# A state-space scan feeding an MLP on one core: exponentials by head, a shorter weight decode, and another order of the MLP's blocks

## The chip, the cores and the metric

The kernel runs on one core of one Trainium2 chip. What counts is the device time of one execution in microseconds. The engines are named as in the profile: PE multiplies matrices, DVE and POOL work elementwise, ACT evaluates functions and copies, SP starts most transfers. PEld is PE's weight load. Each engine works off its own instructions in the order in which they were written; an instruction can wait for others by semaphores, and everything behind it on its engine then waits too.

## What is computed

For each of 4 batches and 8 heads, 768 tokens pass through a scan with a state of 16 x 32 numbers, and the result, rearranged to 3072 tokens of 256 numbers, passes through an MLP with 2048 hidden units:

```
la = log(clip(a, 1e-6, 1)); cum = cumsum(la) within a chunk
L  = exp(cum_i - cum_j) where i >= j, else 0
y  = ((C B^T) * L) x  +  (C state) * exp(cum)
state = exp(cum_last) * state + sum_j exp(cum_last - cum_j) B_j x_j
h  = y @ w_in;   g = h * clip(h + 3, 0, 6) / 6;   out = g @ w_out
```

The two weight matrices are float64 in DRAM. All other inputs and the output are float32.

## The kernel before

The scan uses chunks of 128 tokens instead of the reference's 32, so there are six. Chunk `c` of all four batches makes 512 tokens, and the MLP works through the same 512 tokens as block `k = c`. All tiles have 128 partitions.

*The weights.* They come in eight raw pieces of 1 MB (0 to 3 are `w_in`, 4 to 7 `w_out`), read as pairs of 32-bit words into one of two `raw` buffers. `decode_a` and `decode_b` rebuild a float32 from sign, exponent, and mantissa: `s` is the top 16 bits, `e` the exponent (two biased Relu passes on ACT), `m` the mantissa (scaled on ACT, its low word added on DVE); `decode_b` ends with the product, and asks for the raw piece two further on. Piece i of `w_in` is needed by hidden slices f = 4i to 4i + 3, piece 4 + i of `w_out` by the same slices of the second product.

*The attention part of a chunk* is a generator, `steps(c)`, whose pieces are woven into the MLP of the block before. `ends` makes `bs` (POOL), `eto` (ACT) and `tmp` (POOL); `turn(c, p)` transposes B and C of two batches into `t_ps` and copies them out as `bT` (ACT), `cT` and `csT` (DVE). `decay(c, b)` works on the tile `L`, into which `load_decay` has put the cumulated logs of batch b: POOL subtracts the row's own (L272) and masks (L273), ACT exponentiates (L276). `scores` makes four `cb` tiles on PE and multiplies them into `L` on DVE; `mix` sums into `y`, and `keep` copies `yT` (ACT) and forms the next state (DVE). Chunk 0 needs no transfer for `L`: `diff_first` makes the masked differences in PSUM, in tiles named `d`, with a bf16 mask product (L226), one product per head (L230) and one wide product with `ident_n` (L233), and `decay_first` exponentiates (L242).

*The MLP.* `mlp_in(k, f)` multiplies slice f into an `h` tile (L395), ACT makes `r` (L400), DVE makes slice f of `gT` (L401). One such step is two products in the program and four PE instructions in the trace. `mlp_out(k, b, ...)` sums the 16 slices for batch b into an `o` tile (L409): 16 products, 32 instructions. ACT copies it to `ob`, SP writes it out.

*Order.* It is written by hand: nothing is reordered. The first product of block k is followed by the second product of block k - 1, so two `gT` buffers live at once. Decodes 0 to 2 stand in the opening, 3 and 4 in block 0's first product, 5 to 7 in block 1's. `turn` of the next chunk stands after f = 9 and f = 13, the other pieces between the four `o`.

*Buffers.* PSUM has eight banks. The pool `ps` gives six to `d`, `c_ps`, `t_ps`, `cb`, `h` and `o` in turn, in the order of their making, and two hold `y`. A new tile waits until the readers of the tile that had its bank are done. The tiles `L` and four early ones share five buffers named `big`.

## Time and profile before

| | us |
|---|---|
| median of 3 runs | 473.97 (472.18 to 474.04) |
| profiled execution | 473.95 |
| its span, first to last instruction | 472.2 |
| busy: PE, DVE, ACT, POOL | 445.6, 161.6, 146.4, 75.6 |
| moved by DMA | 30.15 MB |

The span is 1.75 us less than the profiled execution's time; that difference is work around the span. The share of busy time says little here, since a matmul instruction counts as busy for as long as it lasts, and one of the same shape lasts twice as long in some stretches as in others. The chain of waits, read by stretches, says more. Rows of the profile give a line, an engine, an operation, what is written and read, the shape, and a count; in brackets stands how long the engine was idle before, and what ended that.

### The profile page before, as it was taken

To read this page: it belongs to the slowest core of one execution; us is meant where nothing else is said; L and a number is where in the kernel's file an instruction comes from. 1 tells how busy PE (TensorE), PEld (TensorE's weight loads), DVE (VectorE), ACT (ScalarE), POOL (GpSimd) and SP (SyncE) were. 2 spreads that over 40 slices of the span, in tenths; PEclk is the share of its full clock that TensorE was granted. 3 is DMA by queue.
4 is the path that set the end of the run, shared out by engine and by line. 5 is a ranking of instruction groups with operands and counts; after the bars stand their busy time and mean duration, and the time that the engine had idled before them with its cause. 6 is when DMAs were issued, how large, how long until landed. Compare 5 with 4: busy or idle time off the path is not lost.

```text
span 472.2 us, 5101 instructions
## 1 busy us (share of the span) xinstructions
PE 445.6 (94%) x2036; PEld 278.7 (59%) x2036; DVE 161.6 (34%) x291; ACT 146.4 (31%) x225; POOL 75.6 (16%) x63
## 2 busy tenths in 40 slices
PE   5999698999855999999999999999999999999997
PEld 3655343444312778545877446785458774488886
DVE  4514468384639221245121434212451114300000
ACT  5430564637544100345111344003451114400000
POOL 2000009200048000019000057232000000000000
PEclk9999999899985799999999999999999999999999
DMA  8706853148300032620112800326200000000000
GB/s 163 206 4 125 182 161 134 44 178 112 135 0 0 3 104 82 79 70 1 56 58 89 135 0 0 106 77 75 33 1 12 18 17 2 0 11 24 11 24 22
DMA packets 87048, 30.15 MB, mean 64 GB/s; under 512 B 75536, under 2 KB 81360, under 8 KB 87024
## 3 DMA queue, kind: packets, MB, share of 16 engines
q1 hardware_dynamic: 86800, 29.73, 26.3%
q8 instruction: 16, 0.26, 0.2%
q10 hardware_dynamic: 224, 0.10, 0.1%
q14 instruction: 8, 0.07, 0.0%
HBM read 26.57 MB, written 3.24 MB: 63 GB/s over the span
## 4 chain that ended last, share of the span: by engine, by line
PE 81%; issue 8%; DMA 3%; DVE 3%; POOL 2%; ACT 2%; SPq 0%; POOLq 0%; ACTq 0%
PE o L409 36%; PE h L395 26%; PE cb L327 4%; PE d L230 3%; PE y L356 3%; PE d L233 3%; PE y L350 2%; PE y L362 2%; DMA L<-cum_d 1%; POOL L L272 1%; DMA bc<-in_B_dram 1%; PE t_ps L305 1%; PE d L226 1%; DVE w_out L184 1%; DVE gT L401 1%
## 5 line engine op out<-in xcount | busy, mean ns | idle before, releaser
L395 PE MATMUL h<-yT,w_in 128*128 128x512 f32 x384 | 178.4, 619 | 6.6 <-DVE gT L401 5.1
L409 PE MATMUL o<-w_out,gT 128*128 128x256 f32 x768 | 173.5, 385 | 0.0
L409 PEld LDWEIGHTS o<-w_out,gT 128*128 128x128 f32 x768 | 145.9, 192 | 24.4 <-issue 4.1
L395 PEld LDWEIGHTS h<-yT,w_in 128*128 128x128 f32 x384 | 74.2, 198 | 97.5 <-issue 82.1
L401 DVE SCALAR_TENSOR_TENSOR gT<-r,h 128x512 f32<-128x512 f32 x96 | 64.4, 685 | 110.6 <-ACT r L400 110.4
L400 ACT ACTIVATE r<-h,half 128x512 f32<-128x512 f32 x96 | 63.8, 685 | 76.9 <-PE h L395 70.1
L335 DVE TENSOR_TENSOR L<-L,cb 128x256 f32<-128x256 f32 x96 | 33.9, 415 | 104.4 <-PE cb L327 101.2
L414 ACT COPY ob<-o 128x256 f32<-128x256 f32 x24 | 8.9, 372 | 143.1 <-PE o L409 137.6
L272 POOL TENSOR_TENSOR L<-L,cum_t 128x1024 f32<-128x1024 f32 x20 | 39.7, 1987 | 19.6 <-DMA L<-cum_d 19.6
L327 PE MATMUL cb<-cT,bT 32*128 32x256 f32 x192 | 27.9, 484 | 4.2 <-DVE gT L401 3.8
L284 POOL TENSOR_TENSOR bs<-bc,e_from 128x512 f32<-128x512 f32 x5 | 5.3, 1057 | 164.0 <-DMA bc<-in_B_dram 152.0
L276 ACT ACTIVATE L<-L 128x1024 f32<-128x1024 f32 x20 | 21.2, 1061 | 18.4 <-POOL L L273 18.4
L377 ACT COPY yT<-y 128x256 f32<-128x256 f32 x24 | 7.8, 375 | 55.4 <-PE y L362 46.9
L327 PEld LDWEIGHTS cb<-cT,bT 32*128 32x128 f32 x192 | 12.8, 209 | 20.4 <-issue 9.0
L273 POOL TENSOR_SCALAR_AFFINE_SELECT L<-L 128x1024 f32<-128x1024 f32 x20 | 23.6, 1181 | 1.5
L356 PE MATMUL y<-L,xt 128*32 128x128 f32 x384 | 18.4, 303 | 3.1 <-DVE L L335 3.1
L230 PE MATMUL d<-cum,ident 32*128 32x128 f32 x64 | 16.6, 436 | 3.8 <-DVE cum L195 3.8
L230 PEld LDWEIGHTS d<-cum,ident 32*128 32x128 f32 x64 | 14.2, 323 | 8.2 <-DVE cum L195 4.4
L356 PEld LDWEIGHTS y<-L,xt 128*32 128x32 f32 x384 | 10.3, 116 | 8.8 <-DVE L L335 3.9
L233 PE MATMUL d<-ident_n,cum 32*128 32x512 f32 x16 | 15.3, 1056 | 0.0
L293 POOL TENSOR_TENSOR tmp<-state,eto 128x512 f32<-128x512 f32 x4 | 4.2, 1052 | 59.5 <-ACT eto L290 59.5
L380 DVE TENSOR_TENSOR state<-y,mask 128x256 f32<-128x256 f32 x10 | 4.2, 424 | 25.6 <-ACT yT L377 25.6
(58 smaller groups left out, 177.4 us busy)
## 6 DMA issues: line engine op xcount, KB each, us to landing
L<-cum_d SPq DMA_DIRECT2D x20, 512.0 KB, 3.8
raw<-in_moe_w_in_dram SPq DMA_DIRECT2D x4, 1024.0 KB, 5.4
raw<-in_moe_w_out_dram SPq DMA_DIRECT2D x4, 1024.0 KB, 5.4
xt<-in_x_dram SPq DMA_DIRECT2D x6, 512.0 KB, 6.9
out_dram<-ob SPq DMA_DIRECT2D x24, 128.0 KB, 1.7
bc<-in_C_dram SPq DMA_DIRECT2D x6, 256.0 KB, 5.7
bc<-in_B_dram SPq DMA_DIRECT2D x6, 256.0 KB, 7.6
eto<-cum_d SPq DMA_DIRECT2D x40, 32.0 KB, 2.9
```

The source lines that it names most:

```text
L230: nc.tensor.matmul(out=d[:, q], lhsT=ident[:rows, g + q:g + q + 1].to_broadcast([rows, P]), rhs=cum[:, 0], start=False, stop=True, skip_gr ...
L233: nc.tensor.matmul(out=d, lhsT=cum[:, 0], rhs=ident_n[:, g:g + HU].unsqueeze(2).to_broadcast([rows, HU, P]), start=False, stop=True, skip_ ...
L272: nc.gpsimd.tensor_tensor(out=L, in0=L, in1=by_j, op=ALU.subtract)
L273: nc.gpsimd.affine_select(out=L, in_=L, pattern=[[0, NH], [1, P]], compare_op=ALU.is_ge, fill=-1e5, base=0, channel_multiplier=-1)
L276: nc.scalar.activation(L, L, AF.Exp)
L327: nc.tensor.matmul(out=cb.rearrange("j h i -> j (h i)"), lhsT=bT[rows, b % 2], rhs=cT[rows, b % 2].rearrange("n t i -> n (t i)"), start=Tr ...
L335: nc.vector.tensor_tensor(out=L[:, hs], in0=L[:, hs], in1=cbs[q], op=ALU.mult)
L356: nc.tensor.matmul(out=y_ps[u][32 * q:32 * q + 32, k], lhsT=xt[:, b * NH + h], rhs=L[:, h], start=(c == 0), stop=True, tile_position=(0, 3 ...
L395: nc.tensor.matmul(out=h, lhsT=w_in[:, j, f * P:(f + 1) * P], rhs=yTs[k][:, j].rearrange("p b i -> p (b i)"), start=(j == 0), stop=(j == N ...
L400: nc.scalar.activation(r, h, AF.Relu, bias=half, scale=1.0 / 6.0)
L401: nc.vector.scalar_tensor_tensor(out=gTs[k][:, f], in0=r, scalar=1.0, in1=h, op0=ALU.min, op1=ALU.mult)
L409: nc.tensor.matmul(out=o, lhsT=gTs[k][:, f, b * P:(b + 1) * P], rhs=w_out[:, f], start=(f == 0), stop=(f == NF - 1))
```

## The change

The exponentials take the row's own cumulated log as a bias, negated in `cum_n`. In chunk 0 the wide product L233 goes, and 32 passes of 128 x 128 (`decay_exp`) take the place of eight of 128 x 512. In chunk 1, POOL's subtraction goes, and eight such passes for each batch take the place of one of 128 x 1024. Later chunks subtract on POOL as before.

The decode has three parts now. `decode_a` copies `s` and masks `m`, `e` and `s`, and makes the exponent in one Relu pass that writes bf16; `decode_b` merges exponent and sign and adds the low word; `decode_c` multiplies. The mantissa's scaling pass on ACT is gone. Three `raw` buffers hold pieces, and a piece is asked for after `decode_b`. One function table is loaded at the start.

Block k's second product now follows its own first product, so one `gT` buffer serves. Decodes 0 and 1 stand in the opening, 2 to 5 in block 0's first product, 6 and 7 between its first and second. In block 0 the batches 0 and 1 of `o` go together, a piece of `w_out` at a time. Of the eight PSUM banks, four go round among `c_ps`, `t_ps`, `cb` and `h`, two are for `d` and then `o`, and two for `y`. Eight `big` buffers take the place of five. In the opening `by_token` stands ahead of `diff_first`.

```diff
-    ffn = ctx.enter_context(tc.tile_pool(name="ffn", bufs=2))
-    ps = ctx.enter_context(tc.tile_pool(name="ps", bufs=6, space=PSUM))
+    ffn = ctx.enter_context(tc.tile_pool(name="ffn", bufs=1))
+    ps = ctx.enter_context(tc.tile_pool(name="ps", bufs=4, space=PSUM))
+    ps_o = ctx.enter_context(tc.tile_pool(name="ps_o", bufs=2, space=PSUM))
...
-    NRAW = 2
+    NRAW = 3
...
+    load_w(2)
+    nc.scalar.preload_act_table_set("natural_log_exp_and_others")
...
         nc.vector.tensor_scalar(
-            out=e, in0=s, scalar1=4, scalar2=0x7FF,
-            op0=ALU.logical_shift_right, op1=ALU.bitwise_and)
-        nc.scalar.activation(m.bitcast(FP32), m, AF.Copy, scale=2.0 ** -20)
-        nc.scalar.activation(e, e, AF.Relu, bias=bias_hi, scale=-1.0)
-        nc.scalar.activation(e, e, AF.Relu, bias=bias_lo, scale=-float(1 << 7))
+            out=e, in0=s, scalar1=0x7FF0, scalar2=None, op0=ALU.bitwise_and)
+        nc.vector.tensor_scalar(
+            out=s, in0=s, scalar1=0x8000, scalar2=None, op0=ALU.bitwise_and)
+        nc.scalar.activation(e.bitcast(BF16), e, AF.Relu, bias=bias_e, scale=8.0)
...
     def decode_b(i):
...
-            out=m, in0=lo, scalar=2.0 ** -52, in1=m, op0=ALU.mult, op1=ALU.add)
-        nc.vector.tensor_scalar(
-            out=s, in0=s, scalar1=0x8000, scalar2=None, op0=ALU.bitwise_and)
-        nc.vector.tensor_tensor(out=e, in0=e, in1=s, op=ALU.bitwise_or)
+            out=e, in0=e.bitcast(BF16), scalar=255.0 * 2 ** 7, in1=s, op0=ALU.min, op1=ALU.add)
+        nc.vector.scalar_tensor_tensor(
+            out=m.bitcast(FP32), in0=lo, scalar=2.0 ** -32, in1=m, op0=ALU.mult, op1=ALU.add)
+        if i + NRAW < 2 * NP:
+            load_w(i + NRAW)
+
+    def decode_c(i):
...
-        nc.vector.tensor_tensor(out=dst, in0=m, in1=e, op=ALU.mult)
+        nc.vector.scalar_tensor_tensor(
+            out=dst, in0=m, scalar=2.0 ** -20, in1=e, op0=ALU.mult, op1=ALU.mult)
...
+    def decay_exp(c, b, src, h0, n):
+        for q in range(n):
+            g = b * NH + h0 + q
+            nc.scalar.activation(
+                Ls[c, b][:, h0 + q], src[:, q], AF.Exp, bias=cum_n[:, c, g:g + 1])
...
+    weave = {}
+    for i in range(2, 6):
+        for j, part in enumerate((decode_a, decode_b, decode_c)):
+            weave[0, 4 * (i - 2) + j] = part, i
+    for k in range(NC):
+        todo = steps(k + 1) if k + 1 < NC else iter(())
+        for f in range(NF):
+            mlp_in(k, f)
+            if (k, f) in weave:
+                part, i = weave[k, f]
+                part(i)
+            if f in (9, 13):
+                next(todo, None)
+        if k + 2 < NC:
+            load(k + 2)
+        next(todo, None)
+        if k == 0:
+            decode(6)
+            for i in range(NP):
+                for b in range(2):
+                    mlp_out(0, b, i * FP, (i + 1) * FP)
+                if i == 1:
+                    decode(7)
+                if i != 0:
+                    next(todo, None)
+        else:
+            for b in range(2):
+                mlp_out(k, b, 0, NF)
+                next(todo, None)
+            mlp_out(k, 2, 0, NF // 4)
             next(todo, None)
+            mlp_out(k, 2, NF // 4, NF)
+        if k == 0:
+            mlp_out(k, 2, 0, NF)
+        next(todo, None)
+        mlp_out(k, 3, 0, NF)
```

*Three places in the order.* The first is PE's start of the program. `d` is a tile of chunk 0's differences, `c_ps` the transposed logs, `t_ps` the transposed B and C. Before:

```order
L226 MATMUL d<-hide,ident_h 128x512 [waits Pool_49]
L230 MATMUL d<-cum,ident 128x128 [waits DVE_49]
L230 MATMUL d<-cum,ident 128x128 x3
L233 MATMUL d<-ident_n,cum 128x512
L226 LDWEIGHTS ident_h
L226 MATMUL d<-hide,ident_h 128x512
L230 MATMUL d<-cum,ident 128x128 x4
L233 MATMUL d<-ident_n,cum 128x512
L260 MATMUL c_ps<-ident,cum 128x32 x6
L260 MATMUL c_ps<-ident,rest 128x32 [waits DVE_49]
L260 MATMUL c_ps<-ident,rest 128x32 x5
L305 MATMUL t_ps<-ident,bc 128x128 [waits DMAHW2_49]
```

And now:

```order
L263 MATMUL c_ps<-ident,cum 128x32 [waits DVE_49,Pool_49]
L263 MATMUL c_ps<-ident,cum 128x32 x5
L263 MATMUL c_ps<-ident,rest 128x32 [waits DVE_49]
L263 MATMUL c_ps<-ident,rest 128x32 x5
L226 LDWEIGHTS ident_h
L226 MATMUL d<-hide,ident_h 128x512 [waits Pool_49]
L230 MATMUL d<-cum,ident 128x128 x4
L226 LDWEIGHTS ident_h
L226 MATMUL d<-hide,ident_h 128x512
L230 MATMUL d<-cum,ident 128x128 x4
L313 MATMUL t_ps<-ident,bc 128x128 [waits DMAHW2_49]
L313 MATMUL t_ps<-ident,bc 128x128
```

The transposes of `rest`, which wait for DVE, now stand ahead of all `d`, and the wide product is gone from each `d`. The semaphore DMAHW2 is that of the C block's transfer; ACT's fourth write of `cum_d` waits for it too, now, where it waited for another.

The second is ACT around one decode in a first product. `ws`, `we` and `wm` are the decode's s, e and m. Before:

```order
L400 ACTIVATE r<-h,half 128x512 [waits DVE_49,PE_49] x2
L157 COPY ws<-raw 128x1024 [waits DMAHW4_49]
L164 ACTIVATE wm<-wm 128x1024 [waits DVE_49]
L165 ACTIVATE we<-we,bias_hi 128x1024 [waits DVE_49]
L166 ACTIVATE we<-we,bias_lo 128x1024 [waits Activation_49]
L400 ACTIVATE r<-h,half 128x512 [waits PE_49] x3
```

And now, in block 0:

```order
L408 ACTIVATE r<-h,half 128x512 [waits DVE_49,PE_49]
L155 COPY ws<-raw 128x1024 [waits DMAHW4_49]
L163 ACTIVATE we<-we,bias_e 128x1024 [waits DVE_49]
L408 ACTIVATE r<-h,half 128x512 [waits PE_49,Activation_49]
L298 ACTIVATE eto<-eto 128x512 [waits DMAHW4_49,DMAHW5_49,DMAHW3_49,DMAHW6_49,DMAHW2_49,DMAHW7_49,DMAHW1_49,DMAHW0_49]
L317 COPY bT<-t_ps 128x256 [waits PE_49]
L244 ACTIVATE L<-L,cum_n 128x128 [waits DMAHW0_49,Pool_49]
L244 ACTIVATE L<-L,cum_n 128x128 x7
L408 ACTIVATE r<-h,half 128x512 [waits PE_49,Activation_49] x2
```

Of the passes between two `r` two are left; the one on `we` still waits for a mask on DVE, and the next `r` stands behind it. The transposes' copy and eight exponentials stand between other `r`.

The third is PE where the first product of a block after block 0 ends. Before:

```order
L305 MATMUL t_ps<-ident,bc 128x128 [waits DVE_49]
L305 MATMUL t_ps<-ident,bc 128x128 x3
L395 MATMUL h<-yT,w_in 128x512 [waits DVE_49,Activation_49]
L395 MATMUL h<-yT,w_in 128x512
L395 MATMUL h<-yT,w_in 128x512 [waits DVE_49]
L395 MATMUL h<-yT,w_in 128x512
L327 MATMUL cb<-cT,bT 128x256 [waits DVE_49] x3
L327 MATMUL cb<-cT,bT 128x256 [waits DVE_49,Activation_49]
L409 MATMUL o<-w_out,gT 128x256 [waits DVE_49]
```

And now:

```order
L313 MATMUL t_ps<-ident,bc 128x128 [waits DVE_49]
L313 MATMUL t_ps<-ident,bc 128x128 x3
L403 MATMUL h<-yT,w_in 128x512 [waits DVE_49]
L403 MATMUL h<-yT,w_in 128x512
L403 MATMUL h<-yT,w_in 128x512 [waits DVE_49]
L403 MATMUL h<-yT,w_in 128x512
L335 MATMUL cb<-cT,bT 128x256 [waits DVE_49]
L335 MATMUL cb<-cT,bT 128x256 [waits DVE_49,Activation_49]
L335 MATMUL cb<-cT,bT 128x256 [waits DVE_49] x2
L417 MATMUL o<-w_out,gT 128x256 x16
```

The rows look alike, but what the waits mean has moved: with six banks going round, `t_ps` here took the bank of `h` 9 and the four `cb` those of `h` 11 to 13 and of `t_ps`; with four, `t_ps` takes the bank of `h` 10 and the four `cb` those of `h` 13, `t_ps`, `h` 14 and `h` 15. The first `o` waits for nothing of its own.

More of the change, by code (lines that the diff above doesn't have):

```diff
@@ L224, in diff_first @@
             g = b * NH + HU * u
-            d = ps.tile([P, HU, P], FP32, name="d", tag="f")
+            d = ps_o.tile([P, HU, P], FP32, name="d", tag="o")
             nc.tensor.matmul(
@@ L405, in mlp_out @@
         if f0 == 0:
-            outs[k, b] = ps.tile([P, DM], FP32, name="o", tag="f")
+            outs[k, b] = ps_o.tile([P, DM], FP32, name="o", tag="o")
         o = outs[k, b]
@@ L441, in steps, with decode @@
             load_eto(c + 1)
+    def decode(i):
+        decode_a(i)
+        decode_b(i)
+        decode_c(i)
     decode_a(0)
+    by_token()
     diff_first(0)
-    by_token()
     turn(0, 0)
-    decode_b(0)
     decay_first(0)
     turn(0, 1)
+    decode_b(0)
+    decode_c(0)
     ends(0)
     diff_first(1)
-    decode_a(1)
     scores(0, 0)
     decay_first(1)
+    decode_a(1)
     diff_first(2)
@@ L464 @@
     keep(0, 0)
-    decode_a(2)
     decay_first(3)
-    load(1)
-    load_eto(1)
+    decode_c(1)
     scores(0, 3)
@@ L472 @@
     keep(0, 1)
+    load(1)
+    load_eto(1)
     for b in range(NB):
         load_decay(1, b, nc.sync)
[L475 to L489 removed]
```

77 lines of the change are left out of this document (20 added, 57 removed).

## The prediction

> **What bounds the kernel now.** I read the profile by stages first: busy time in each stretch between landmarks of the chain (start of the first `h` product, of block 2's, of block 3's). Columns: stretch, length, busy time of PE, PEld, DVE, ACT, POOL, granted clock, DMA share.
>
> ```profile
> 0.00:57.84 57.84, 48.06 (x220) 28.34 (x221) 22.01 (x45) 22.25 (x30) 5.37 (x16) 1.00 0.62 135
> 57.84:192.75 134.91, 121.30 (x529) 65.92 (x530) 70.14 (x115) 54.97 (x78) 30.47 (x19) 0.90 0.30 86
> 192.75:257.75 65.00, 65.00 (x330) 41.61 (x329) 19.95 (x40) 18.18 (x31) 13.93 (x10) 1.00 0.27 61
> 322.74:386.26 63.52, 63.52 (x314) 40.81 (x313) 18.51 (x36) 18.52 (x31) 0.00 (x0) 1.00 0.17 25
> ```
>
> From 192.75 us PE never rests, and the order of a block is all that could change there. The losses lie earlier. The chain of waits (start, length, what, instructions) gives the paces:
>
> ```profile
> 10.07 0.54 PE d L226
> ...
> 12.61 1.71 PE d L233 x2
> 14.31 1.23 PE c_ps L260 x12
> 15.54 1.90 PE t_ps L305 x8
> ...
> 36.58 1.01 PE y L356 x16
> 37.59 0.63 PE y L362 x4
> ...
> 81.65 6.51 PE h L395 x8
> ...
> 154.49 9.36 PE o L409 x32
> ...
> 192.75 17.17 PE h L395 x40
> 209.92 0.44 PE t_ps L305 x4
> 210.35 6.87 PE h L395 x16
> ...
> 228.85 0.64 PE cb L327 x8
> ...
> 230.85 7.10 PE o L409 x32
> ...
> 413.73 55.27 PE o L409 x256
> ```
>
> An `h` instruction takes 6.51/8 = 0.81 us at 81.65 and 17.17/40 = 0.43 at 192.75: PE has a half pace and a full pace, and the granted clock (1.00 in the first stretch) doesn't show which. At full pace a block is 27.5 of `h` (64 instructions), 4 x 7.1 of `o`, and 9 of attention. The stretch 57.84 to 192.75 holds two `h` (54.9), one `o` (28.4) and two attention parts (18), 101.3 us; it took 134.9, so 33.6 went into waits and half pace. These are the waits:
>
> ```profile
> 115.60 1.28 DVE L401 SCALAR_TENSOR_TENSOR gT<-r,h 128x512 f32<-128x512 f32 x2 [3.58 <-ACT r L400]
> 126.80 3.70 PE L395 MATMUL h<-yT,w_in 128*128 128x512 f32 x8 [1.28 <-DVE gT L401]
> 136.66 0.66 PE L305 MATMUL t_ps<-ident,bc 128*128 128x128 f32 x4 [3.22 <-DVE gT L401]
> 148.23 2.80 DVE L184 TENSOR_TENSOR w_out<-wm,we 128x1024 f32<-128x1024 f32 x1
> ```
>
> With each weight piece decoded, `gT` waits 3.58 us behind three ACT passes, and PE behind `gT`. After a wait of 1.28 PE kept full pace (3.70/8 = 0.46); the 3.22 was followed by slow instructions.
>
> **The opening, to the first `h`: 57.84 becomes 48.3.** Each of eight `d` tiles loses its L233 pair (1.71 of 14.31 - 10.07 = 4.24) and keeps 2.53. PE is the chain almost throughout, so 13.7 us could go. But three new orders give some back. Prices not yet shown (line, operation, count, total and mean ns):
>
> ```profile
> L254 DVE TENSOR_TENSOR rest<-cum 32x768 f32<-32x768 f32 x1 | 0.9, 937 | 0.0
> L161 DVE TENSOR_SCALAR we<-ws 128x1024 uint16<-128x1024 uint16 x8 | 3.4, 422 | 2.0 <-ACT ws L157 2.0
> L242 ACT ACTIVATE L<-d 128x512 f32<-128x512 f32 x8 | 4.4, 591 | 8.4 <-PE d L233 8.4
> L400 ACT ACTIVATE r<-h,half 128x512 f32<-128x512 f32 x96 | 63.8, 685 | 76.9 <-PE h L395 70.1 <-DVE gT L401 6.8
> L377 ACT COPY yT<-y 128x256 f32<-128x256 f32 x24 | 7.8, 375 | 55.4 <-PE y L362 46.9 <-PE y L356 8.5
> ```
>
> First, `by_token` now stands ahead of the `d` tiles on PE, and its `rest` stands on DVE behind two masks of decode 0, which wait for ACT's `ws` copy; ACT's fourth `cum_d` write now waits for the landing of the C block. Rows of the timeline, a score group's (needed below) among them, and the answer on the C block's tile:
>
> ```profile
> 1.71 0.46 SPq L84 DMA_DIRECT2D bc<-in_C_dram  x1
> 7.97 1.09 ACT L157 COPY ws<-raw 128x1024 uint16<-128x1024 uint16 x1 [3.52 <-DMA cum_d<-cum]
> 49.13 1.24 PE L327 MATMUL cb<-cT,bT 32*128 32x256 f32 x8
> DMA to landing us min/median/max: 7.1/7.1/7.1
> ```
>
> That is 1.71 + 7.1 = 8.8, `ws` to 10.4 instead of 9.1, two masks (0.84) and `rest` (0.94) to 12.2, half of c_ps to 12.8. Then two `d` (5.1) to 17.9 and the transposes (1.9) to 19.8. Second, the exponentials: eight of 128x128 with a bias instead of two of 128x512, which no row shows. Bounds: 256 columns cost 0.375 and 512 cost 0.591, so 0.86 ns a column; continuing down, and less the overlap of neighbours of 0.1 (a `yT` pair takes 0.65), gives 0.16 apart; the top is 0.375, a 256-wide one unoverlapped. I take 0.25, since the biased `r` costs 0.09 more than the unbiased L242. PE may go on when batch 0's first four are done, 18.9 + 0.4 (`bT`) + 1.0 = 20.3. From there its queue is six `d` (15.2), four score groups, three `y` groups at 1.01 + 0.63: 45.4. Third, `yT` of the first pair now precedes batch 3's eight exponentials on ACT: the copies end at 43.3, exponentials at 45.4, the last score products near 46.5, the last `y` 47.4, `yT` 48.1. With hand-overs 48.3, so -9.5.
>
> [...]
>
> Off the path, costing nothing: the table load (before c_ps ACT has nothing on the chain), the lost constants, the raw pieces (three buffers: each lands well before its decode), `load(k+2)` one phase earlier. `load(1)` and the decays are queued on SP behind raw piece 4, which decode 1 releases before 40 us; they are read after 73. If that cover went, a landing (7.1 for the C block) would be paid once.
>
> **Block 0: 48.3 to 130.6.** Remaining prices:
>
> ```profile
> L401 DVE SCALAR_TENSOR_TENSOR gT<-r,h 128x512 f32<-128x512 f32 x96 | 64.4, 685 | 110.6 <-ACT r L400 110.4
> L158 DVE TENSOR_SCALAR wm<-raw 128x1024 uint32<-128x1024 uint32 x8 | 5.6, 695 | 0.4 <-DMA raw<-in_moe_w_in_dram 0.4
> L172 DVE SCALAR_TENSOR_TENSOR wm<-raw,wm 128x1024 f32<-128x1024 uint32 x8 | 9.7, 1217 | 0.0
> L311 DVE TENSOR_TENSOR cT<-t_ps,parity 128x512 f32<-128x512 f32 x12 | 8.2, 685 | 1.5 <-ACT bT L309 1.2
> L317 DVE TENSOR_TENSOR csT<-t_ps,eto 128x256 f32<-128x256 f32 x10 | 4.1, 413 | 0.0
> L293 POOL TENSOR_TENSOR tmp<-state,eto 128x512 f32<-128x512 f32 x4 | 4.2, 1052 | 59.5 <-ACT eto L290 59.5
> L273 POOL TENSOR_SCALAR_AFFINE_SELECT L<-L 128x1024 f32<-128x1024 f32 x20 | 23.6, 1181 | 1.5
> ```
>
> A decode now has two ACT passes where it had four, the second priced like `ws` (1.09, the same 1024 16-bit elements), and on DVE two masks, `wm`, and three scalar_tensor_tensor passes, the 16-bit one not in the trace: below, the 0.69 of a 16-bit tensor_tensor (timeline, us):
>
> ```profile
> 118.39 0.69 DVE L176 TENSOR_TENSOR we<-we,ws 128x1024 uint16<-128x1024 uint16 x1
> ```
>
> above, L172's 1.22. I take 1.22, the same operation. Neighbours overlap by 0.08 (two `gT` in 1.28). PE needs 6.9 us for four `h`, DVE more, so DVE sets this phase. Its period: `gT` 0.62, `wm` 0.60, mask 0.42, then the wait for ACT's new pass and the `r` queued behind it (1.09 + 0.69 and 0.12 of hand-overs = 1.9, the second mask inside it), `gT` 0.62, two passes 2.28, `gT` 0.62, pass 1.14, `gT` 0.62: 8.8.
>
> The first `gT` starts four slow `h` (3.3) and an `r` (0.9) after 48.3, at 52.5. Two periods bring `gT` 8 to 70.1. In the third, `r` 9 ends at 73.6; behind it stand on ACT `eto` (0.6, a 512-wide pass), a wait for POOL's `tmp` and select (1.05 + 1.18; the subtraction that stood between them is now the bias), eight exponentials (2.1) and `r` 10 (0.69): `gT` 10 at 79.4, `gT` 12 at 81.8. In the fourth, `gT` 13 at 85.3, two passes, `cT` and `csT` (3.4), `gT` 14, pass, `gT` 15 to 91.7. The fourth score tile takes the bank of `h` 15, so PE waits for that, slow by then: 92.5. The sixteen program matmuls of `o` (32 instructions) at 154.49's price, 9.4: 101.9. Scores and `y`, 230.85 - 228.85 = 2.0; `o` 3.55; 2.0; 3.55; 2.0; 7.1; `y` 1.4; 7.1: 130.6. Decodes 6 and 7 follow on DVE behind four score products (1.6, at `csT`'s price): 0.6 + 0.42, a wait of 1.2 for ACT, 3 x 1.14 = 5.7 each, so they end near 100 and 105.5. PE wants them at 103.9 and 109.5: about 4 us of cover, and an overrun is paid in full. Before, the same work with its share of losses took 64.9 + 33.6, now 82.3: -16.2.
>
> **Blocks 1 to 4: +7.0.** `o` now follows its own `h`, and the common banks are four. The second transposes take the bank of `h` 10, whose `gT` is late behind the decay chain:
>
> ```profile
> 216.30 2.40 ACT L400 ACTIVATE r<-h,half 128x512 f32<-128x512 f32 x4
> ```
>
> `r` 10 starts there, `gT` 10 ends 0.72 + 0.65 later, 217.7; `h` 13 ends at 209.92 + 0.44 + 6.87 = 217.2: PE waits about 0.6. The fourth score tile waits for `gT` 15: 0.05 + 0.72 + 0.69 after `h` 15, then 0.4, less the 0.64 the scores took: +1.3. For the last attention part there is no `tmp`, so only 1.3. In all 3 x 1.9 + 1.3 = 7.0; nothing if banks came free earlier.
>
> **Sum against the profiled execution** (span 472.2, time 473.95, so 1.75 around it; the runs' median is 473.97): 130.6 + 3 x (65.0 + 1.9) + (63.5 + 1.3) + 27.5 + 27.6 (half of 55.27) + 3.2 (469.0 to 472.2) = 454.4, and 1.75 more: 456.
>
> **Rivals.** *Pace lost on the way, 466*: PE's half pace comes back in block 0's second half, where DVE leaves it waits of up to 1.7 us: eight `h` cost up to 6 more; or POOL's tiles hold DVE as at 148.23 (2.80 against 1.22) for three passes, +4.7. For: 136.66. Against: 126.80, and the eight L172 passes average 1.22, POOL or not. *No cost in blocks 1 to 4 and cheap passes, 448*: -7.0, and 4 x 0.5 for a 16-bit pass at 0.69. Against: the order shows the waits. *Full pace in the opening, 449*: 20 us of PE work there would halve, but ACT and DVE (22 us each in the first stretch) then set it, leaving about -7. The rows speak against it: PE worked from 10 to 47 us with hardly a gap and `d` never sped up. [...] *Slower, 484*: in blocks 1 to 4 the two waits and the narrow score products between them drop PE to half pace, and one `o` (7.1) is run slowly in each: +28. It decides from +18, 4.5 us a block. For: 3.22 sufficed at 136.66; against: mine are 0.6 and 1.5, and 1.28 did not.
>
> **How the numbers follow.** Forecast 0.60; pace lost 0.16; no cost 0.10; full pace 0.06; slower 0.05; the rest, 0.03, a stall I missed that eats the gain. The bounds: exponentials -1.8 to +2.5 (twenty on the path), the pass -2, the first two rivals -9 and +10. Range 447 to 468. Less than 0.5% (2.4 us) can't be told from no change; faster 0.92, same 0.03, slower 0.05.
>
> **What would show it.** Right: the first `h` at 47 to 50 us; `gT` in block 0's `h` phase 8.8 us per four; block 1's `h` near 130; blocks 1 to 3 about 66.9 each, with PE waiting on `gT` before the last `cb`. Wrong: `d` under 2.5 us a tile; blocks at 65.0; `h` at 0.8 us in block 0 after 60 us; decode 6 or 7 released later than `o` asks for it.

## The result, and the profile after

The changed kernel takes 457.3 us (median of four runs, 456.8 to 457.6); the kernel before took 473.1 beside it (471.9 to 474.0). The ratio is 0.967, with a 95% interval of 0.964 to 0.970. The forecast was 456, with a range of 447 to 468. The profiled execution has a span of 455.6 us.

Busy time by stages, cut at the first `h` of blocks 0 to 5 (columns as in the prediction):

```profile
0.00:47.22 47.22, 33.93 (x204) 23.27 (x205) 21.87 (x41) 17.14 (x45) 4.32 (x15) 1.00 0.80 149
47.22:129.45 82.23, 74.16 (x328) 45.60 (x329) 50.85 (x77) 35.66 (x71) 9.32 (x7) 0.92 0.58 120
129.45:197.00 67.55, 66.11 (x329) 41.83 (x328) 19.95 (x40) 18.29 (x31) 13.90 (x10) 1.00 0.34 59
331.98:397.05 65.07, 64.21 (x313) 41.09 (x312) 18.52 (x36) 18.52 (x31) 0.00 (x0) 1.00 0.03 9
397.05:455.60 58.55, 55.26 (x193) 36.29 (x191) 11.01 (x16) 12.85 (x21) 0.00 (x0) 0.99 0.04 12
```

| stage | forecast | measured |
|---|---|---|
| opening, to the first `h` | 48.3 | 47.2 |
| block 0 | 82.3 | 82.2 |
| blocks 1 to 3, each | 66.9 | 67.5 |
| block 4 | 64.8 | 65.1 |
| rest | 58.3 | 58.6 |

So the parts came out nearly as the sum, and part of that is luck: inside the first two stages errors of 1 to 2.5 us cancel. What PE waits for in the changed kernel (total us, times, longest):

```profile
PE c_ps L263 <- DVE rest L257: 5.8, 1, 5.8
PE cb L335 <- DVE gT L409: 4.7, 5, 1.2
PE h L403 <- DVE csT L325: 3.1, 1, 3.1
PE t_ps L313 <- DVE gT L409: 2.5, 4, 0.9
```

The first is the opening's new order, `rest` ahead of `d`. The second and fourth are the two bank waits: in blocks 1 to 4 `cb` waits four times, 3.5 us in all, and `t_ps` three times, 1.6 us in all; block 0 has one of each, and these are the longest (1.2 and 0.9). The third, in block 0, was not in the sum. The timeline of the changed kernel at these places (start, length, engine, line; in brackets the idle time before and its end). In the opening:

```profile
10.06 1.09 ACT L155 COPY ws<-raw 128x1024 uint16<-128x1024 uint16 x1 [5.60 <-DMA cum_d<-cum]
16.84 2.07 PE L230 MATMUL d<-cum,ident 32*128 32x128 f32 x8
20.26 2.18 ACT L244 ACTIVATE L<-d,cum_n 128x128 f32<-128x128 f32 x8
47.22 17.50 PE L403 MATMUL h<-yT,w_in 128*128 128x512 f32 x40 [0.47 <-ACT yT L385]
```

`d` keeps its slow 2.07 us, eight exponentials take 2.18 (0.27 apart), and the first `h` runs at 0.44 per instruction at once; the prediction had the first four `h` slow. At the ends of block 0's second and third groups of four `h`:

```profile
62.00 0.69 DVE L409 SCALAR_TENSOR_TENSOR gT<-r,h 128x512 f32<-128x512 f32 x1 [1.33 <-ACT r L408]
62.60 1.22 DVE L169 SCALAR_TENSOR_TENSOR we<-we,ws 128x1024 uint16<-128x1024 bf16 x1
...
70.61 0.69 DVE L409 SCALAR_TENSOR_TENSOR gT<-r,h 128x512 f32<-128x512 f32 x1 [1.33 <-ACT r L408]
71.18 1.05 POOL L301 TENSOR_TENSOR tmp<-state,eto 128x512 f32<-128x512 f32 x1 [21.45 <-ACT eto L298]
71.22 2.09 DVE L169 SCALAR_TENSOR_TENSOR we<-we,ws 128x1024 uint16<-128x1024 bf16 x1
72.18 6.20 POOL L278 TENSOR_SCALAR_AFFINE_SELECT L<-L 128x1024 f32<-128x1024 f32 x4
73.23 2.10 DVE L171 SCALAR_TENSOR_TENSOR wm<-raw,wm 128x1024 f32<-128x1024 uint32 x1
76.41 3.75 PE L403 MATMUL h<-yT,w_in 128*128 128x512 f32 x4 [3.07 <-DVE csT L325]
```

The period of the groups is 70.61 - 62.00 = 8.61 us (forecast 8.8), and the 16-bit pass takes 1.22 as chosen. But beside POOL's `tmp` and selects it and the next pass take 2.09 and 2.10, and POOL's first two selects take 2.08 and 2.06 where the other two, which begin with no such pass running, take 1.09. PE then waits 3.07 us for `csT`, and four instructions take 3.75. In block 1:

```profile
152.25 1.06 ACT L282 ACTIVATE L<-L 128x1024 f32<-128x1024 f32 x1 [3.97 <-POOL L L278]
153.22 2.41 ACT L408 ACTIVATE r<-h,half 128x512 f32<-128x512 f32 x4
154.66 0.66 PE L313 MATMUL t_ps<-ident,bc 128*128 128x128 f32 x4 [0.58 <-DVE gT L409]
160.46 0.69 PE L335 MATMUL cb<-cT,bT 32*128 32x256 f32 x2 [0.86 <-DVE gT L409]
161.09 1.13 PE L417 MATMUL o<-w_out,gT 128*128 128x256 f32 x4
```

Both predicted waits are there. Four `r` queue up behind an exponential that waited 3.97 us for POOL.

### The profile page after: what moved, and what is told of

The parts are those of the page before. It is cut to its first block, busy times and chain, and to the rows that moved or that the text cites. A ratio compares the mean times of both kernels' runs of the same rounds, so it can differ in the third digit from the quotient of the medians.

```text
span 455.6 us, 5119 instructions
## 1 busy us (share of the span) xinstructions
PE 425.9 (93%) x2020; PEld 271.7 (60%) x2020; DVE 162.1 (36%) x289; ACT 139.0 (31%) x260; POOL 66.2 (15%) x59
## 4 chain that ended last, share of the span: by engine, by line
PE 66%; issue 14%; SPq 5%; DVE 5%; ACT 3%; POOL 3%; DMA 3%; ACTq 0%; POOLq 0%
PE o L417 35%; PE h L403 18%; PE cb L335 3%; SPq L215 3%; PE d L230 3%; PE y L364 2%; DVE gT L409 2%; PE y L358 2%; DMA eto<-cum_d 1%; ACT r L408 1%; POOL L L277 1%; SPq L85 1%; POOL L L278 1%; PE y L370 1%; PE t_ps L313 1%
## 5 line engine op out<-in xcount | busy, mean ns | idle before, releaser
L403 PE MATMUL h<-yT,w_in 128*128 128x512 f32 x384 | 171.2, 602 | 4.9 <-DVE csT L325 3.1
L403 PEld LDWEIGHTS h<-yT,w_in 128*128 128x128 f32 x384 | 72.7, 193 | 92.3 <-issue 83.7
L277 POOL TENSOR_TENSOR L<-L,cum_n 128x1024 f32<-128x1024 f32 x16 | 30.3, 1895 | 14.9 <-DMA L<-cum_d 14.9
L335 PE MATMUL cb<-cT,bT 32*128 32x256 f32 x192 | 25.1, 474 | 6.2 <-DVE gT L409 4.7
L335 PEld LDWEIGHTS cb<-cT,bT 32*128 32x128 f32 x192 | 11.2, 205 | 17.9 <-DVE gT L409 9.9
L282 ACT ACTIVATE L<-L 128x1024 f32<-128x1024 f32 x16 | 17.0, 1063 | 11.8 <-POOL L L278 11.8
L364 PE MATMUL y<-L,xt 128*32 128x128 f32 x384 | 17.3, 297 | 0.0
L163 ACT ACTIVATE we<-we,bias_e 128x1024 bf16<-128x1024 uint16 x8 | 9.2, 1148 | 16.6 <-DVE we L159 16.6
```

The costliest lines, as they stand in the source:

```text
L277: nc.gpsimd.tensor_tensor(out=L, in0=L, in1=by_j, op=ALU.add)
L282: nc.scalar.activation(L, L, AF.Exp)
L335: nc.tensor.matmul(out=cb.rearrange("j h i -> j (h i)"), lhsT=bT[rows, b % 2], rhs=cT[rows, b % 2].rearrange("n t i -> n (t i)"), start=Tr ...
L364: nc.tensor.matmul(out=y_ps[u][32 * q:32 * q + 32, k], lhsT=xt[:, b * NH + h], rhs=L[:, h], start=(c == 0), stop=True, tile_position=(0, 3 ...
L403: nc.tensor.matmul(out=h, lhsT=w_in[:, j, f * P:(f + 1) * P], rhs=yTs[k][:, j].rearrange("p b i -> p (b i)"), start=(j == 0), stop=(j == N ...
```

## The experiments

Twelve kernels. Each was timed against the kernel before on its own chip (470 to 474 us); "to the change" is the ratio's difference from 0.9667 times 472.3 us, and is good to about 2 us to either side. First `h` and block lengths are read from the starts of the blocks' first `h` in each trace.

| kernel | us | ratio to before (95%) | to the change, us | first `h` | block 0 | blocks 1 to 3 |
|---|---|---|---|---|---|---|
| the change | 457.32 | 0.967 (0.964 to 0.970) | 0 | 47.2 | 82.2 | 67.5 |
| e1_scores_later | 450.35 | 0.954 (0.951 to 0.956) | -6.1 | 47.3 | 82.1 | 65.95 |
| e2_scores_turn_later | 449.98 | 0.954 (0.953 to 0.955) | -6.0 | 47.6 | 81.5 | 65.8 |
| e3_d_first | 451.06 | 0.956 (0.953 to 0.959) | -5.1 | 42.1 | 81.1 | 67.5 |
| e4_relu_later | 455.91 | 0.964 (0.961 to 0.967) | -1.4 | 47.9 | 81.0 | 67.5 |
| e5_exps_alone | 459.87 | 0.973 (0.970 to 0.976) | +3.0 | 46.6 | other order | 65.0 |
| e6_no_mask_chunk1 | 454.41 | 0.961 (0.959 to 0.964) | -2.6 | 47.3 | 78.9 | 67.5 |
| e8_old_decode | 461.28 | 0.978 (0.975 to 0.980) | +5.2 | 45.6 | 87.7 | 67.5 |
| e9_full_rows | 447.80 | 0.947 (0.944 to 0.950) | -9.3 | 38.7 | 81.3 | 67.5 |
| e10_four_edits | 434.76 | 0.920 (0.917 to 0.924) | -21.9 | 35.4 | 81.7 | 65.0 |
| e11_five_edits | 437.77 | 0.928 (0.924 to 0.932) | -18.4 | 36.7 | 81.9 | 65.0 |
| e12_six_edits | 433.86 | 0.918 (0.915 to 0.922) | -22.8 | 39.8 | 76.0 | 65.0 |
| e13_scores_first | 427.25 | 0.907 (0.902 to 0.912) | -28.2 | 34.6 | 74.1 | 65.0 |

### What each part of the change is worth

**The exponentials alone**, in the kernel before, chunk 0 only:

```diff
-            nc.tensor.matmul(
-                out=d, lhsT=cum[:, 0],
-                rhs=ident_n[:, g:g + HU].unsqueeze(2).to_broadcast([rows, HU, P]),
-                start=False, stop=True, skip_group_check=True)
...
-            nc.scalar.activation(L[:, HU * u:HU * u + HU], diffs.pop((b, u)), AF.Exp)
+            d = diffs.pop((b, u))
+            for q in range(HU):
+                g = b * NH + HU * u + q
+                nc.scalar.activation(
+                    L[:, HU * u + q], d[:, q], AF.Exp, bias=cum_n[:, 0, g:g + 1])
```

> The kernel before with one part of the change alone: in chunk 0 the exponentials run per head with the negated cum as bias, and the second broadcast product of each d tile is dropped. Theory (the opening is bound by TensorE, which loses 13.7 us of products and gains some of it back in longer exponentials): the first h starts at 45 to 46 instead of 57.8, the rest of the trace is unchanged: -12, about 460 us. Rival (a pass that waits for C or the decode's queue keeps PE waiting): the first h at 50 or later, 464 us or more.

459.9 us, 12.7 less than the kernel before (ratio 0.973). The first `h` moves from 57.84 to 46.59 us, which is even earlier than in the full change:

```profile
46.59 11.19 PE L396 MATMUL h<-yT,w_in 128*128 128x512 f32 x20 [0.47 <-ACT yT L378]
```

So dropping L233 alone gives as much as the whole change does in the opening. The rest of the change gives and takes there about equally: its order of `d` costs 5.1 us (e3 below), and the change without that order starts its first `h` at 42.10, 4.5 before this kernel. What gives these 4.5 us was not told apart. Of the 14.8 us by which the span shrank (472.2 to 457.4), 11.25 lie before the first `h`. Between the first `h` and block 2's the stretch also fell, from 134.75 to 131.1; the granted clock over it is 0.93 instead of 0.90. What made it so is not shown.

**The old decode** in the new places (three ACT passes on mantissa and exponent instead of one, the sign merged in `decode_b`, and a plain last product):

```diff
-        nc.scalar.activation(e.bitcast(BF16), e, AF.Relu, bias=bias_e, scale=8.0)
+        nc.scalar.activation(m.bitcast(FP32), m, AF.Copy, scale=2.0 ** -20)
+        nc.scalar.activation(e, e, AF.Relu, bias=bias_hi, scale=-1.0)
+        nc.scalar.activation(e, e, AF.Relu, bias=bias_lo, scale=-float(1 << 7))
```

> The changed kernel with the decode's operations as before the change (three ScalarE passes of a half instead of one, and the last multiplication a plain one), at the places in block 0 where the change put it. Theory (VectorE sets the pace of block 0's h, four groups of 8.6 us): ScalarE's relu for r and the passes queue behind each other, a group takes 1.7 to 1.9 us more, and the first decodes in the opening end later: +7 to +10, 465 to 467 us. Rival (only the weaving of the decode into block 0 and the order of its products shortened block 0, the leaner operations are covered): 457.

+5.2 us, under the range. The mechanism and its size hold; in this kernel's timeline `gT` waits as before the change, and the period is 10.34:

```profile
53.54 0.69 DVE L413 SCALAR_TENSOR_TENSOR gT<-r,h 128x512 f32<-128x512 f32 x1 [3.58 <-ACT r L412]
63.88 0.69 DVE L413 SCALAR_TENSOR_TENSOR gT<-r,h 128x512 f32<-128x512 f32 x1 [3.58 <-ACT r L412]
```

That is 1.73 more per group; from the first `gT` to the first `o` the sum is 6.5. Then 1.0 comes back among the `o`. The expected loss in the opening was a gain of 1.6: only one mask stands ahead of `rest` there instead of two, and the first `ws` copy began at 8.88 us instead of 10.06, because the C block landed earlier (below).

### The two bank waits of blocks 1 to 4

```diff
-            for b in range(2):
-                mlp_out(k, b, 0, NF)
-                next(todo, None)
+            mlp_out(k, 0, 0, NF // 4)
+            next(todo, None)
+            mlp_out(k, 0, NF // 4, NF)
+            next(todo, None)
+            mlp_out(k, 1, 0, NF)
```

The `next(todo)` that stood ahead of these is left for block 0 alone.

> The changed kernel, with the fourth product cb of a chunk's first batch in blocks 1 to 4 issued behind the first quarter of batch 0's output products instead of ahead of them. Theory (it waits for the bank of the last h, that is for gT15, and the emptied pipe costs TensorE more on top): the step from the last h to the first o falls from 2.19 us to about 0.7, and blocks 1 to 4 are shorter by about 1.5 us each: -6, about 451 us. Rival (the new order of a block, both products in a row through one g buffer, lengthens it whatever the scores wait for): blocks 1 to 3 stay 67.5 long and the time stays at 457.

-6.1 us, as the theory had it. The stages of this kernel:

```profile
129.44:195.44 66.00, 65.43 (x330) 41.56 (x329) 20.07 (x40) 18.29 (x31) 13.90 (x10) 1.00 0.35 61
327.32:390.83 63.51, 63.51 (x313) 40.82 (x312) 18.63 (x36) 18.52 (x31) 0.00 (x0) 1.00 0.03 9
```

Each block is 1.55 shorter, and block 4 is back at its 63.5 of before. The new order of a block costs nothing by itself; the bank does.

The second edit moved the second transposes from f = 13 to f = 14 as well:

> As the run before, and in blocks 1 to 4 the second pair of transposes behind the sixteenth group of h less one (f = 14 instead of 13), so that it takes a bank whose gT is long done. Theory: the wait of t_ps for gT10 (0.6 us, and 0.2 twice in the refilled pipe) goes as well, blocks 1 to 3 are back at about 65.0 us as before the change and block 4 at about 63.5: -9, about 448.4 us. Rival (the transposes then wait for the next gT at their new place): no better than the run before, about 451.

The rival held: no better. At the new place the next `h` waits as long for the same `gT`:

```profile
154.27 1.99 PE L403 MATMUL h<-yT,w_in 128*128 128x512 f32 x4 [0.57 <-DVE gT L409]
```

So the place isn't the cause, and the bank only passes the lateness on. What is late is `r` 10, behind an exponential that waits for POOL. That reading was tried in the kernel of four edits, below.

### The opening

`d` of batch 0 back ahead of `by_token`:

```diff
-    by_token()
     diff_first(0)
+    by_token()
     turn(0, 0)
```

> The changed kernel with the first two d products issued ahead of the products by token instead of behind them, as before the change. Theory (the opening's PE is the bound from 12.98 us on, and 5 us of d products fit into its idle time before): the first h starts about 5 us earlier, at 42 instead of 47.2, about 452.3 us. Rival (the opening is bound by ScalarE's exponentials or by the arrival of data, so that the d products are only waited for elsewhere): 0 to -1.5, 456 to 457.

-5.1 us, and the first `h` at 42.10, so the theory held: PE does two `d` in time in which it otherwise waits for `rest`.

```profile
6.29 2.07 PE L230 MATMUL d<-cum,ident 32*128 32x128 f32 x8 [3.77 <-DVE cum L195]
```

Next the pace itself. `cum` is padded with zero rows, so each `d` product is contracted over 128 rows instead of 32, with as many columns to stream and the same result:

```diff
-    cum = big([NB * NH, NC, P], "cum")
+    cum_z = big([P, NC, P], "cum")
+    nc.vector.memset(cum_z, 0.0)
+    cum = cum_z[:R]
...
-                    out=d[:, q], lhsT=ident[:rows, g + q:g + q + 1].to_broadcast([rows, P]),
-                    rhs=cum[:, 0], start=False, stop=True, skip_group_check=True)
+                    out=d[:, q], lhsT=ident[:, g + q:g + q + 1].to_broadcast([P, P]),
+                    rhs=cum_z[:, 0], start=False, stop=True, skip_group_check=True)
```

> The changed kernel with the d products of chunk 0 contracted over 128 rows (cum padded with zero rows, added by one memset) instead of 32. The same columns stream. Theory (the slow pace of the opening comes from the few rows, not from pauses): after about 4 us of them the products run at full pace, a d tile's four products take 1.0 instead of 2.0 us, and the first h starts 5 to 8 us earlier, 448 to 451 us. Rival (pauses set the pace, or it doesn't depend on the rows): d stays at 2.0 and the first h at 47, 456 us on this chip.

-9.3 us, a little beyond the theory. Rows of the timeline:

```profile
14.55 1.91 PE L233 MATMUL d<-cum,ident 128*128 128x128 f32 x8
16.68 1.41 PE L233 MATMUL d<-cum,ident 128*128 128x128 f32 x8
20.25 1.05 PE L233 MATMUL d<-cum,ident 128*128 128x128 f32 x8
38.67 11.85 PE L406 MATMUL h<-yT,w_in 128*128 128x512 f32 x27 [0.47 <-ACT yT L388]
```

The third tile already takes half the time, and the first `h` starts 8.55 us earlier. With 32 rows `d` stayed at 2.07 for 26 us of almost unbroken work. So the rows decide here, not the pauses.

### Block 0

The exponent pass of pieces 2 and 3 behind the next `r` instead of ahead of it:

```diff
-        nc.scalar.activation(e.bitcast(BF16), e, AF.Relu, bias=bias_e, scale=8.0)
         halves[i] = s, e, m
+    def decode_r(i):
+        s, e, m = halves[i]
+        nc.scalar.activation(e.bitcast(BF16), e, AF.Relu, bias=bias_e, scale=8.0)
```

> The changed kernel with the exponent pass of pieces 2 and 3 on ScalarE (its relu with bias_e) issued one product h later, behind that h's relu r, so that r does not wait for it. Theory (in the first two groups of block 0 VectorE stands idle for 1.33 us because r queues behind the exponent pass, and VectorE sets the pace): both groups fall from 8.6 to about 7.3 us, -2.7, about 453 us on this chip if the changed kernel is at 456. Rival (TensorE's 7.0 us for four h, or the collision with GpSimd in the third group, takes the gain back): 0 to -1.

Between theory and rival: the two groups take 8.0 instead of 8.6, 0.6 each and not 1.33. The pass now stands ahead of the `r` after next, and half of the idle time is found there:

```profile
54.03 0.69 DVE L412 SCALAR_TENSOR_TENSOR gT<-r,h 128x512 f32<-128x512 f32 x1 [0.75 <-ACT r L411]
62.04 0.69 DVE L412 SCALAR_TENSOR_TENSOR gT<-r,h 128x512 f32<-128x512 f32 x1 [0.73 <-ACT r L411]
```

The time, -1.4 us, lies within its uncertainty, so not even its sign is shown.

POOL's selects of chunk 1 left out:

```diff
-        nc.gpsimd.affine_select(
-            out=L, in_=L, pattern=[[0, NH], [1, P]], compare_op=ALU.is_ge,
-            fill=-1e5, base=0, channel_multiplier=-1)
         if c > 1:
+            nc.gpsimd.affine_select(
+                out=L, in_=L, pattern=[[0, NH], [1, P]], compare_op=ALU.is_ge,
+                fill=-1e5, base=0, channel_multiplier=-1)
```

> The changed kernel without GpSimd's causal selects in chunk 1 (the mask of chunk 1 is left out, so its positions above the diagonal are not hidden). Theory (the selects of 6.2 us stretch VectorE's two decode passes beside them from 1.22 to 2.1 us each and keep the exponentials waiting, and TensorE, 3.07 us idle at csT, then runs h at half pace): the two passes are back at 1.22, the wait for csT falls below 1.5, the half pace is gone, and block 0 is 3 to 5 us shorter: 451 to 453 us on this chip. Rival (the stretch has another cause, such as ScalarE or the DMA traffic of that moment): passes stay at 2.1 and the time at 456.

-2.6 us, block 0 3.3 shorter. In this kernel's timeline:

```profile
71.30 1.05 POOL L301 TENSOR_TENSOR tmp<-state,eto 128x512 f32<-128x512 f32 x1 [21.29 <-ACT eto L298]
71.34 2.08 DVE L169 SCALAR_TENSOR_TENSOR we<-we,ws 128x1024 uint16<-128x1024 bf16 x1
73.35 1.21 DVE L171 SCALAR_TENSOR_TENSOR wm<-raw,wm 128x1024 f32<-128x1024 uint32 x1
75.64 1.96 PE L403 MATMUL h<-yT,w_in 128*128 128x512 f32 x4 [1.06 <-ACT r L408]
```

L171 is back at 1.21, and `csT` comes 0.77 us earlier (75.08 instead of 75.85). The theory expected more of it. PE's wait fell to 1.06 mainly because PE had come there later: it ran twelve `h` in 7.11 us, partly at half pace, where the change took 3.70 for eight and 1.98 for four. The four `h` behind the wait, 1.96 us instead of 3.75, give another 1.8, and four `h` in e4 took 1.96 behind an undiminished wait of 3.07 (see the last section), so how much of the 3.3 us the selects are to blame for stays open. L169 still takes 2.08: of POOL's work only `tmp` runs beside it, which the theory had overlooked. Eight exponentials of ACT begin beside it as well, but beside eight others in this trace the same pass takes 1.22 (at 81.75). So `tmp` holds up a DVE pass too, by 0.87 us for its own 1.05.

### The edits together

The rows, the order of `d`, the later scores, and, new, ACT's exponentials one turn later than POOL's part of the same `L`:

```diff
         turn(c, 0)
-        decay(c, 0)
+        decay_pool(c, 0)
         yield
         turn(c, 1)
-        decay(c, 1)
+        decay_act(c, 0)
+        decay_pool(c, 1)
         yield
+        decay_act(c, 1)
```

> Four edits of the changed kernel together: the d products over 128 rows, the first two d ahead of the products by token, the fourth cb of blocks 1 to 4 behind the first quarter of batch 0's output products, and in every chunk ScalarE's exponentials of a batch issued one turn later than GpSimd's part (add and select) of the same L, so that no relu r queues behind an exponential that waits for GpSimd. Theory (the waits are apart from each other, so the gains add): opening -8.6 by the rows and another -3 by the order, -6.2 by the scores, and the wait of t_ps for gT10, which comes from r being behind such an exponential, goes too (blocks 1 to 3 at 65.0 instead of 65.95, -2.9): 435 to 438 us on a chip where the changed kernel takes 456. Rival 1 (the opening is at its next bound, ScalarE's and VectorE's queue, with the rows alone): the order gives nothing, 438 to 441. Rival 2 (t_ps waits for another reason than the exponentials): blocks 1 to 3 stay at 65.95, +2.9.

434.8 us, 21.9 below the change and just under what the theory gave; both rivals fell. The first `h` starts at 35.35 (38.67 with the rows alone), and blocks 1 to 3 are as long as before the change, with PE busy throughout:

```profile
117.08:182.07 64.99, 64.99 (x329) 41.59 (x328) 20.33 (x40) 18.67 (x31) 13.91 (x10) 1.00 0.35 62
```

So the wait for `gT` 10 came from the exponentials' place on ACT.

Then piece 2 of the weights into the opening, to relieve DVE in block 0:

```diff
     decay_first(3)
-    decode_c(1)
     scores(0, 3)
+    decode_c(1)
+    decode_a(2)
     mix(0, 2)
     mix(0, 3)
     keep(0, 1)
+    decode_b(2)
...
+    weave[0, 0] = decode_c, 2
-    for i in range(2, 6):
+    for i in range(3, 6):
         for j, part in enumerate((decode_a, decode_b, decode_c)):
-            weave[0, 4 * (i - 2) + j] = part, i
+            weave[0, 4 * (i - 3) + 1 + j] = part, i
```

> As the run before, and piece 2 of the weights decoded at the end of the opening, ahead of the first gT, instead of in the first four groups of h; pieces 3 to 5 follow from the second h on. Theory (VectorE's passes set the pace of block 0's h, 7.3 us of them for a piece; three of the four passes of piece 2 then run while VectorE is idle): block 0 is 4 to 5 us shorter than in the run before. Rival (the passes delay the last scores and copies of the opening, or the collision with GpSimd moves onto other passes): 0 to 2 us.

Slower than the four edits, by 3.0 us. From the first `h` to the first `o` it takes 38.8 us instead of 43.0, the 4.2 expected, and three places give more than that back:

```profile
36.69 19.13 PE L413 MATMUL h<-yT,w_in 128*128 128x512 f32 x40 [2.74 <-ACT yT L395]
85.14 3.72 PE L427 MATMUL o<-w_out,gT 128*128 128x256 f32 x16 [0.48 <-DVE w_out L185]
91.26 1.79 PE L345 MATMUL cb<-cT,bT 32*128 32x256 f32 x8 [2.39 <-DVE L L353]
```

`yT` stood behind the piece's exponent pass on ACT, and `h` ran slowly after that pause of 2.74 us (19.13 us for forty instructions, 17.50 in the change); pieces 6 and 7, behind sixteen exponentials on ACT, came too late for `w_out` and for the scores behind them on DVE. The next kernel moved these: the first part of piece 2 behind `decode_b(1)`, that of piece 6 ahead of chunk 1's last exponentials, piece 7 right behind 6. Against the changed kernel:

```diff
     decode_b(1)
+    decode_a(2)
...
     decode_c(1)
+    decode_b(2)
     scores(0, 3)
...
+            decode_a(6)
             next(todo, None)
-            decode(6)
+            decode_b(6)
+            decode_c(6)
+            decode(7)
```

> As the run with piece 2 decoded in the opening, with that piece's first part further ahead (behind the second part of piece 1, where ScalarE is idle for 3.0 us, so that the copies yT don't queue behind its exponent pass), piece 6's first part ahead of the last exponentials of chunk 1, and piece 7 right behind piece 6. Theory (the earlier run lost what block 0's h phase gained, 4.2 us, to yT, 2.3, and to pieces 6 and 7, which came late behind 16 exponentials on ScalarE and let TensorE wait for w_out and for the scores): the first h is back at 35.3 to 36, the h phase keeps its gain, the waits for w_out and the scores go, and the time is 3 to 4.5 us below the kernel of four edits, 430 to 432. Rival (VectorE's passes for pieces 2 to 7 are the bound of block 0 as a whole, so what is moved within it comes back elsewhere): 434 to 436.

433.9 us: block 0 is 5.7 shorter than with four edits, the opening 4.5 longer. That was an oversight in the order: `scores(0, 3)` now stood behind three passes on DVE, and `y` waited for it.

```profile
37.08 1.64 PE L374 MATMUL y<-L,xt 128*32 128x128 f32 x16 [2.48 <-DVE L L353]
```

The last kernel puts it back:

```diff
+    scores(0, 3)
     decode_c(1)
     decode_b(2)
-    scores(0, 3)
```

> As the run before, with the last scores of chunk 0 ahead of the last part of piece 1 and the second of piece 2, where they had stood behind 3.6 us of those passes on VectorE. Theory (the run before lost in its opening what it gained in block 0, 4.5 against 5.7 us, because y waited 2.48 us for these scores and TensorE fell to half pace behind the pause): the first h starts at 35.5 to 36.5 instead of 39.8, block 0 keeps 76 to 77, and the time is 429 to 431. Rival (the passes are then late for the first gT and the first h waits instead): 433 to 435.

427.3 us, ratio 0.907 (0.902 to 0.912): 6.6 us below the one before by the medians, 5.4 by the ratios, and about 2 below the range expected. The first `h` starts at 34.59 and keeps full pace, 17.43 us for forty instructions where the one before took 19.44; block 0 is shorter by as much:

```profile
34.59 17.43 PE L413 MATMUL h<-yT,w_in 128*128 128x512 f32 x40 [0.47 <-ACT yT L395]
```

This is the fastest of the kernels, some 28 us below the change and 45 below the kernel before.

## Why the prediction held, step by step

**The opening.** Forecast -9.5, measured -10.6. The drop of L233 is a sufficient cause (e5), and the steps that give back were right: `rest` late (`d` from 13.8 on, forecast 12.8), and the exponentials at 0.27 instead of 0.25. The reason given for the late `ws` copy held too, with the landing mis-sized: the C block landed 8.0 us after its issue at 1.72, so at 9.72, not after 7.1, and ACT issued the fourth write of `cum_d` at 9.74. In the row shown above the profile names a write of `cum_d`, but in e1 the same row names the C block:

```profile
10.17 1.09 ACT L155 COPY ws<-raw 128x1024 uint16<-128x1024 uint16 x1 [5.72 <-DMA bc<-in_C_dram]
```

In all kernels with this wait the fourth write follows that landing by 0.02 to 0.03 us; in e8 the C block landed at 8.54. Why it is later in the others stays open. At the third `d` tile the kernel was 1.1 us later than forecast (21.46 against 20.3). It was made up because the score groups, among `d` products, cost 0.85 us instead of 1.24 (two `d` and a group take 27.37 - 21.46 = 5.91, less twice 2.53), and because the last `y` were already running faster: four L370 took 0.70 us at 41.88, 0.57 at 44.69 and 0.44 at 46.31, and the first clock record of this trace, at 45.0 us, is one of full clock. The prediction's reading that the granted clock doesn't show the pace goes too far. It doesn't in the opening, where the trace has no record and the view counts full clock; after the first record it does in the stretches compared here: 0.81 us per `h` at 81.65 in the kernel before, under a clock of 0.50, and 0.43 at 192.75 under 1.00.

**That the order of `d` is free was never asked.** The prediction priced the two `d` behind `by_token` at 5.1 us on the path, correctly (e3: -5.1), as part of the change's cost.

**Block 0.** Forecast 82.3, measured 82.2, by two errors. *The first `h` at half pace* failed: the first `gT` came 2.7 us after the first `h`, not 4.2, with `h` at 0.44 us per instruction from its start. *POOL beside DVE* failed the other way. The prediction argued that L172's mean of 1.22, "POOL or not", spoke against a stretch; of the eight passes behind that mean only the last met POOL, and there POOL was the one held up (below). This is a part of the rival "pace lost": 1.75 us in two passes and 0.3 in a third (L185, 1.51 at 77.94), a wait of 3.07, and half pace behind it. Without the selects block 0 is 3.3 us shorter (e6), a third of that rival's price, and part of that is the pace. The period per group, the choice of 1.22 for the 16-bit pass, the ACT passes that were spared (e8: 1.73 a group), and the cover of pieces 6 and 7 held.

**Blocks 1 to 4.** Both waits were found where the order showed them, with the right sources. The size was short: 7.0 forecast, 9.1 measured (three times 2.5 and 1.55). The waits themselves are 0.58 and 0.86, near the forecast, but a wait costs more than its length: without the second a block is 1.55 shorter (e1), without the first another 0.95 (65.95 to 65.0, e10). The sum had 1.3 and 0.6.

**The rivals.** *No cost in blocks 1 to 4* fell by e1: the cost is real, and can be ordered away. *Full pace in the opening* didn't happen, but its price (-7) is close to what e9 gets for it (-8.6), once the products have all rows. *Slower* fell: after waits of 0.6 to 0.9 us PE kept its pace, the granted clock stayed at 1.00, and PE was busy for 0.75 or more of each 3.41 us step of the clock's records in which they lie (last section).

## What to carry to other kernels

Where few PSUM banks go round, look up for each new tile which tile had its bank and which engine reads that last, and look then for what stands ahead of this reader on its own engine; here one exponential that waited 3.97 us for GpSimd made a matmul two engines away 0.58 us late. A pass moved into idle time is free only if its place on every engine's queue is ahead of nothing urgent: in e4, e11 and e12 the gain of one stage was lost, in part or whole, at the first instruction queued behind. When a stretch of matmuls runs at half pace, look at the number of contracted rows before the gaps: here a tile of `d` took 2.07 us over 32 rows and 1.05 over 128. Then compare gaps of equal length: four `h` behind 3.07 us of waiting took 3.75 in one kernel and 1.96 in another.

## What the runs showed of the hardware

**In the opening the pace went with the rows.** Products over 32 rows stayed at 2.07 us a tile of `d` for all of the changed kernel's opening. With 128 rows (e9) the tiles that began at 14.55, 16.68 and 20.25 us took 1.91, 1.41 and 1.05; PE had worked without a break from 13.38 to 18.97. The granted clock reads 1.00 over the changed kernel's opening, but its trace has no clock record before 45.0 us, so the view doesn't show the clock under which the slow products ran. Why the rows matter was not shown.

**In two traces the clock's records change in steps of 3.41 us, and the same wait was followed by half pace in one kernel and by full pace in another.** In the changed kernel's trace the granted clock is 1.00 from 45.01 us, 0.50 from 75.73, 1.00 from 82.56, 0.50 from 89.38, and 1.00 from 96.21 to 454.61. In the kernel before it is 1.00 from 63.44, 0.50 from 80.51, 1.00 from 87.34, 0.50 from 138.54, and 1.00 from 159.02 to 473.04. All these stretches are whole multiples of 3.413 us: 9, 2, 2, 2 and 105 of them, and 5, 2, 15, 6 and 92. Four `h` instructions behind 3.07 us of waiting took 3.75 us in the changed kernel and 1.96 in e4, with the same wait for the same tile. Steps around the wait (columns as above, the granted clock third from the end), first of the change:

```profile
72.31:75.73 3.42, 1.03 (x3) 0.19 (x1) 3.42 (x3) 1.44 (x5) 3.42 (x2) 1.00 0.00 0
75.73:79.14 3.41, 2.73 (x4) 1.21 (x5) 2.33 (x4) 3.41 (x8) 2.65 (x3) 0.50 0.64 204
```

And of e4:

```profile
68.00:71.42 3.42, 1.98 (x6) 0.68 (x5) 2.06 (x4) 2.50 (x4) 0.79 (x1) 1.00 0.56 207
71.42:74.83 3.41, 1.37 (x4) 0.30 (x2) 3.41 (x3) 1.09 (x4) 3.41 (x3) 1.00 0.00 1
74.83:78.24 3.41, 2.38 (x8) 1.16 (x8) 2.33 (x4) 3.41 (x9) 3.00 (x3) 1.00 0.60 152
```

In the change most of the wait fell into one step, with PE busy for 1.03 us of it, and the clock fell at its end. In e4 it reached into two steps, with PE busy for 1.37 and 2.38 us, and the clock stayed. The two traces with their records listed above have three more falls before the end of the work: PE was busy for 0.35 of the step before 89.38 in the change, and for 0.87 and 0.39 of those before 80.51 and 138.54 in the kernel before; the step with 0.87 holds products over 32 rows. Steps with PE busy for 0.65 (from 65.49 in the change) and 0.51 (from 131.71 in the kernel before) were not followed by a fall, and neither was e4's with 0.40. What decides was not shown. Nor does the length of a wait tell by itself: behind waits of 0.88 and 1.07 us twelve `h` took 7.11 us in e6, and behind 0.89 and 1.08 eight took 3.70 in the change. What this is worth in block 0 is not shown either: of the change's four executions the one with the highest mean clock (0.993) took 457.59 us, the others (0.984 and 0.985) 456.83 to 457.35.

**DVE and GpSimd passes took longer beside each other.** L169 on DVE grew from 1.22 to 2.08 us beside one POOL operation of 1.05 us that had begun 0.04 us ahead of it (e6). In the kernel before, the one L172 pass that met POOL had begun first, and POOL's operation grew from 1.90 to 2.86 (timeline):

```profile
143.45 1.22 DVE L172 SCALAR_TENSOR_TENSOR wm<-raw,wm 128x1024 f32<-128x1024 uint32 x1
143.56 2.86 POOL L272 TENSOR_TENSOR L<-L,cum_t 128x1024 f32<-128x1024 f32 x1
```

In these two pairs the one that began second is the one that took longer. In the change, where two DVE passes and POOL's operations followed each other closely from 71.18 us on, both sides did: the passes took 2.09 and 2.10 instead of 1.22, the first two selects 2.08 and 2.06 instead of 1.09. What they share was not shown.
